# A gated attention kernel on one core: an up product moved ahead of the attention, the second Q moved behind the first scores, and the x pieces of the second half issued at other times

## The chip, the core and the metric

The kernel runs on one core of one Trainium2 chip. The core has four compute engines that work side by side: TensorE (PE, the matrix products), VectorE (DVE), ScalarE (ACT) and GpSimd (POOL); SyncE (SP) issues most of the transfers between the chip's main memory (DRAM) and the core's memory (SBUF). Products are written to PSUM, in banks of 128 x 512 numbers. Each engine takes its instructions strictly in the order in which they were written for it, and waits when the next one isn't ready.

The metric is the device time of one execution in microseconds, the median of several runs. The kernel before has 1978.97 us (three runs, 1977.46 to 1979.05).

## The reference

Input x is 2048 rows of 640. It is normalised by rows (xn), and the output is `x + s * g`:

```python
xn = _layernorm(x, axis=-1)
# s: 32 heads of 128, the last W = 512 keys and values of a cache of 2048
q = (xn @ wq); p = softmax(q @ k.T * 128**-0.5); s = concat_heads(p @ v) @ wo
# g: an MLP of width 1728 with a squared ReLU, then SiLU
h = xn @ w1 + b1; r = where(h > 0, h, 0); g = silu((r * r) @ w2 + b2)
```

All is done in float32. Every product of two float32 matrices is made of three products of shorter parts (hi x hi, hi x lo, lo x hi): the code calls that a triple. A part is made by a rounding copy (hi) and a subtraction (lo).

## The kernel before

The 2048 rows are four tiles of 512 columns (`NT`); 640 is five chunks of 128 (`DC`), 1728 is fourteen chunks f of up to 128 (`FC`). The work has three stages.

**The MLP of tiles 0 to 2** (`mlp_step`, L379). For each tile and chunk f: five triples of the up product, ReLU on ACT, square on POOL, split on ACT and DVE, then five triples of the down product. `gate` (L369) ends a tile. The normalised, split x of every tile is stored in DRAM (`xT_d`) for the attention.

**The attention** runs in 128 units: two halves of two tiles, each half with 16 groups of two heads, each group with two tiles, so four units to a group. For unit i:

- `q_mm` (L487): Q, 15 products from x (`ax`) and `wq` into a bank `pq`; `q_hi` and `q_lo` split it. Q is made two units ahead (`AHEAD`).
- `s_mm` (L510): scores, 12 products into four banks `s`.
- `max_fold`, `gather`, `row` (L521 to L553): maxima over the keys on DVE (`rdm`), gathered by ACT, reduced by DVE to `rowm`; SP stores the row as `m_d` in DRAM and reads it back as a broadcast to 128 partitions, `bm`.
- `shift` (L555): DVE subtracts `bm` from the scores in four steps and frees the four banks; the result is `e`. `expo`, `p_hi`, `p_lo` make exp and its parts `pt` (ACT, POOL), `s_add` the sum `su` (POOL, between the two `pt`).
- `s_fold`, `gather`, `row`: the sums, the same way with `rds`, `s_d` and the broadcast `bs`.
- `v_mm` (L588): 12 products into the only bank `o`; `o_norm` (DVE, times `bs`), `o_hi`, `o_lo` make `ot`. `r_mm` (L612) multiplies by `wo`, after every second unit, and `r_acc` adds up.

One unit comes to 54 products in the steady course.

**The MLP of tile 3** is spread over the rest. Chunks 11 to 13 are *early*: their up product (`early_up`, L727) is put among the first four units, with weights and x still in SBUF; `late_relu`, `late_square` (on DVE here) and `early_split` make h, which SP stores in DRAM (`h_d`) and reads back at the end (`late_h`, L749). Chunks 0 to 10 are *late*: weights are loaded and split again (`late_load`, `late_prep`), up products `late_up` and down products `late_down` are put among and after the last units, and for the five output columns d the down products of the early chunks, `late_gate` and the store end the kernel.

**The order is written out by hand.** Every step of the attention and of the late stage is put in a list by `at(when, step)` (L863), with a planned time; unit i starts at i times 12.4 (`PERIOD`). The list is sorted by planned time, and this gives each engine its order, SP's queue of transfers too. The planned times set the order alone; nothing waits for them.

The x of the second half (10 pieces of 256 KB a tile, two parts by five chunks) is loaded by L881 to L888 while the first half ends. Each tile takes over the SBUF room of a tile of the first half after that tile's last Q. The first tile's first use is the Q of unit 64, made in unit 62; the second tile's is the Q of unit 66, in unit 64.

Names in the profile: `eu` are the early products, `lu` and `ly` the late up and down products, `lr` the ReLU's result, `eh_x` and `eh_g` the two parts of an early h, `lh` the parts of h in the late stage, `l1w`, `l2w` its weights. Most instructions are recorded under line 72, that of a helper, so groups are told apart by these names.

Of the kernel before, what the change touches and what calls it, by code (L numbers as in the profile page):

```python
# [8 lines left out]
F32 = mybir.dt.float32  # L9
# [5 lines left out]
P = 128  # L15
NT = 512
# [4 lines left out]
def kernel(  # L21
# [62 lines left out]
    ]  # L84
    g_d = [dpool.tile([P, DC, NT], F32, name=f"g_d{t}") for t in range(LATE)]
    s_d = [dpool.tile([P, DC, NT], F32, name=f"s_d{t}") for t in range(NTILE // 2)]
    h_d = {f: dpool.tile([P, 2, NT], F32, name=f"h_d{f}") for f in range(FC - 3, FC)}

    def raw(ap):
        return ap.bitcast(F32)  # L90
# [7 lines left out]

    psx = ctx.enter_context(tc.tile_pool(name="psx", bufs=1, space=PSUM))

    FA = FC - 3
    keep = ctx.enter_context(tc.tile_pool(name="keep", bufs=1))
    mctx, wctx, hctx = ExitStack(), ExitStack(), ExitStack()
    wpa = wctx.enter_context(tc.tile_pool(name="mwa", bufs=1, side="right"))
# [5 lines left out]

    w1s, w2s = [], []
    for f, (f0, n) in enumerate(chunks):
        wp = wpa if f < FA else wpb
        if n < P:
            w1s.append([wp.tile([P, DC, 2 * n], F32R, name=f"w1s{f}")])
        else:
            if f < FA - 1:
                w1p = [wp.tile([P, DC, n], F32R, name=f"w1s{f}_{i}") for i in range(2)]
            else:
                two = keep.tile([P, 2, D], F32R, tag="ot", name=f"w1s{f}", bufs=4)  # L120
                w1p = [two[:, i, :].rearrange("p (c n) -> p c n", n=n) for i in range(2)]
            w1s.append(w1p)
        w2s.append([wp.tile([P, D], F32R, name=f"w2s{f}_{i}") for i in range(2)])
# [322 lines left out]
    def bank(name, k):  # L446
        return pools["psa"].tile([P, NT], F32, tag=f"qr{k}", name=name, bufs=1)
# [39 lines left out]
    def q_mm(i, cs):  # L487
        hf, g, t, h = units[i]
        if 0 in cs:
            QPS[i] = bank(f"pq{i}", int(i != 1))  # L490
        ws, xs = WQ[hf, h], XT[hf, t]
        for c in cs:
            triple(
                QPS[i],
                (ws[0][:, c, :], ws[1][:, c, :]),
                (xs[0][:, c, :], xs[1][:, c, :]),
                c == 0,
                c == DC - 1,
            )

    def q_hi(i):
        Q[i] = pair("q", [P, NT], f"q{i}", AHEAD + 1)
        act.activation(Q[i][0], QPS[i], AF.Copy, scale=SCALE)
# [243 lines left out]
            sp.dma_start(h_d[f][:, k, :], raw(h))  # L747

    def late_h(f):  # L749
        kind, bufs = ("wv", G) if f < FC - 1 else ("q", AHEAD + 1)  # L750
        LH[f] = pair(kind, [P, NT], f"lh{f}", bufs)
        for k in range(2):
            sp.dma_start(raw(LH[f][k]), h_d[f][:, k, :])

    def late_relu(f, kind):
        n = chunks[f][1]
# [55 lines left out]
        store(sp, HALF - 1, TPH - 1, d, a)  # L812

    steps_n = len(steps)
    opened = (LATE - 1) * FC + FA
    for n in range(steps_n):
        mlp_step(n)
        if n == opened:
# [28 lines left out]
            :, :NT  # L847
        ],
    )
    q_mm(1, range(DC))  # L850
    q_hi(1)
    q_lo(1)
    mctx.close()
    ap = ctx.enter_context(tc.tile_pool(name="at", bufs=2))
    pools["psb"] = ctx.enter_context(tc.tile_pool(name="psb", bufs=1, space=PSUM))
# [7 lines left out]
    def at(when, f, *a):  # L863
        plan.append((max(when, 0.0), len(plan), f, a))
# [14 lines left out]
                    at(base + when, prep, kind, hf, h)  # L879
    at(10.0, pad, pools["ep"], 480)  # L880
    for t in range(TPH):  # L881
        for c in range(DC):
            k, late = divmod(c + 1 - t, 2)
            w = (NG * UPG + t * G - 3 - AHEAD + t + k) * PERIOD + (8.5 if late else -1.6)
            if c == 0:
                at(w, open_xT, 1, t)
            for i in range(2):
                at(w + 0.7 * i, load_xT, 1, t, i, slice(c, c + 1))  # L888
    R_AT = (
        ((2 * PERIOD + 11.25, range(G)),),  # L890
        ((3 * PERIOD + 2.75, range(G)),),
# [9 lines left out]
    for i in range(NU):  # L901
# [5 lines left out]
        hf, g, t, h = units[i]  # L907
        for c in range(KC):
            on(0.68 * c, s_mm, i, c)
        if i + AHEAD < NU:  # L910
            q_at = 3.45 if i % G and i > UPG else 4.3
            for c in range(DC):
                on(q_at + 0.68 * c, q_mm, i + AHEAD, (c,))
            on(q_at + 3.5, q_hi, i + AHEAD)
            on(q_at + 4.1, q_lo, i + AHEAD)
        for c in range(KC):
            on(0.8 + 0.68 * c, max_fold, i, c)
        on(3.95, gather, i, "m")
# [40 lines left out]
    for item in order:  # L959
        kind, n = item[0], int(item[1:] or 0)  # L960
        if kind == "u":
            UP_AT[n] = now
        elif kind == "d":
            DOWN_AT[n] = now
            at(now, late_down, n, range(DC))
        elif kind == "r":
            at(now, r_mm, NU - 1, n, range(G), (n + 1) % 2)
            at(now + 1.36, r_acc, NU - 1, n)
        else:
            for k, d in enumerate(range(DC)):  # L970
                for f in range(FC - 3, FC):
                    DOWN_AT.setdefault(f, now)
                    at(now + 0.68 * (3 * k + f - FC + 3), late_down, f, (d,))
                at(now + 2.04 * (k + 1), late_gate, d)
        now += STEP[kind]
    PREP = {
        0: z - 2 * PERIOD + 8.4,
# [31 lines left out]
    for f, u in sorted(DOWN_AT.items()):  # L1009
# [3 lines left out]
        at(PREP2[f], late_prep, 2, f)  # L1013
        if f >= FA:
            at(now - 8.0 - 4.0 * (FC - f), late_h, f)
    EARLY_IN = (0,) * 7 + (1,) * 3 + (2,) * 3 + (3,) * 2
    for n, u in enumerate(EARLY_IN):
        k, c = divmod(n, DC)
        f = FA + k
        at(u * PERIOD + 8.0 + 0.01 * n, early_up, f, k % 2, c)  # L1020
        if c == DC - 1:
            at(u * PERIOD + 10.6, late_relu, f, "s")
            at(u * PERIOD + 12.0, late_square, f, dve)
            at((u + 1) * PERIOD + 7.6, early_split, f)
    at(z + 2.0, late_x)
    for d in range(DC):
# [51 lines left out]
```

## Time and profile before

| what | before |
|---|---|
| median of three runs | 1978.97 us |
| the profiled execution | 1978.84 us |
| its span, first to last instruction | 1977.1 us |
| PE busy | 1952.0 us (99%) |
| DVE, POOL, ACT busy | 1534.0, 1379.6, 1186.0 us |
| DRAM traffic over the span | 111 GB/s |
| granted TensorE clock, mean | 0.999 |

The page of the profile gives totals; the timeline gives every instruction with its start, its length, and in brackets how long its engine stood idle before it and for what. Engine names with a q (SPq) are the queues that issue transfers: the length there is that of issuing, not of moving the data. A stage view gives, for a stretch of the span, each engine's busy time and the rate at which the transfers moved data. A product of 512 columns is shown with 389 ns, but such products overlap; their distance is shorter.

### The profile page before, as it was taken

How to read it: one execution, taken by the hardware profiler on the slowest of the kernel's cores; microseconds unless marked ns; L12 is line 12 of the kernel's file. 1: busy time of each engine (PE TensorE's matmuls, PEld its weight loads, DVE VectorE, ACT ScalarE, POOL GpSimd, SP SyncE). 2: the span in 40 equal slices, each digit the busy share in tenths (PEclk: the TensorE clock that was granted, in tenths of full speed). 3: DMA queues.
4: the chain of work that ended last, by engine and by line, in shares of the span. 5: the costliest groups of instructions: out<-in, count | busy, mean ns of one | idle time of the engine just before them, and what ended most of it. 6: DMA issues, size and time to landing. Idle time of an engine off the chain costs nothing.

```text
span 1977.1 us, 25595 instructions
## 1 busy us (share of the span) xinstructions
PE 1952.0 (99%) x8576; PEld 1607.7 (81%) x8576; DVE 1534.0 (78%) x2638; ACT 1186.0 (60%) x2035; POOL 1379.6 (70%) x763
## 2 busy tenths in 40 slices
PE   7999999999999999999999999999999999999998
PEld 6888887888888888888887788888888888888877
DVE  5533336788888888888888878888888888888864
ACT  4432326766666666666666676666666666666643
POOL 2121225888888888888887788888888888888841
PEclk9999999999999999999999999999999999999999
DMA  5431444333233333333335533333333333323454
GB/s 150 125 112 33 181 178 147 107 91 91 92 92 91 91 93 90 95 92 92 91 97 166 160 97 107 113 114 115 112 114 113 113 112 113 97 91 92 110 156 133
DMA packets 128917, 220.35 MB, mean 111 GB/s; under 512 B 23590, under 2 KB 38352, under 8 KB 127504
## 3 DMA queue, kind: packets, MB, share of 16 engines
q1 hardware_dynamic: 125792, 204.28, 34.3%
q0 software_dynamic: 2992, 14.43, 1.8%
q8 instruction: 67, 1.10, 0.2%
q14 instruction: 66, 0.54, 0.1%
HBM read 194.26 MB, written 24.39 MB: 111 GB/s over the span
## 4 chain that ended last, share of the span: by engine, by line
PE 87%; DVE 5%; DMA 4%; ACT 2%; issue 1%; POOL 0%; SPq 0%; DVEq 0%; ACTq 0%; POOLq 0%
PE r L72 20%; PE pq L72 20%; PE o L72 16%; PE s L72 16%; PE ph L95 2%; PE ph L97 2%; PE ph L96 2%; PE py L96 2%; PE py L95 2%; PE py L97 2%; PE ly L72 2%; PE lu L72 1%; DMA w1r<-in_w_dram 1%; DVE acc L72 1%; DMA bm<-m_d 1%
## 5 line engine op out<-in xcount | busy, mean ns | idle before, releaser
L72 POOL TENSOR_TENSOR pt<-e,pt 128x1024 fp32r<-128x1024 f32 x256 | 616.3, 2407 | 128.7 <-ACT pt L72 101.9
L72 PE MATMUL r<-ot,wo 128*128 128x512 f32 x1920 | 497.0, 389 | 0.3 <-DVE acc L72 0.3
L72 PE MATMUL pq<-ax,wq 128*128 128x512 f32 x1920 | 456.5, 389 | 0.8 <-DMA ax<-xT_d 0.6
L72 PEld LDWEIGHTS pq<-ax,wq 128*128 128x128 f32 x1920 | 360.4, 188 | 76.2 <-DMA ax<-xT_d 1.5
L72 PEld LDWEIGHTS r<-ot,wo 128*128 128x128 f32 x1920 | 360.3, 188 | 75.8 <-DVE acc L72 0.7
L72 PE MATMUL s<-q,wk 128*128 128x512 f32 x1536 | 369.6, 389 | 4.6 <-DVE e L72 4.6
L72 PE MATMUL o<-pt,wv 128*128 128x512 f32 x1536 | 371.1, 390 | 0.8 <-DVE ot L72 0.5
L72 ACT ACTIVATE e<-e 128x1024 f32<-128x1024 f32 x256 | 269.7, 1053 | 136.7 <-DVE e L72 116.7
L72 DVE TRANSPOSE_TENSOR_REDUCE rdm<-s 128x16 f32<-128x512 f32 x512 | 343.0, 707 | 3.0 <-PE s L72 2.9
L72 PEld LDWEIGHTS s<-q,wk 128*128 128x128 f32 x1536 | 288.0, 188 | 66.3 <-DVE e L72 6.0
L72 PEld LDWEIGHTS o<-pt,wv 128*128 128x128 f32 x1536 | 287.3, 188 | 64.5 <-DVE ot L72 2.9
L72 DVE TENSOR_TENSOR e<-s,bm 128x512 f32<-128x512 f32 x512 | 312.5, 666 | 18.4 <-DMA bm<-m_d 18.2
L72 POOL TENSOR_TENSOR su<-e,e 128x1024 f32<-128x1024 f32 x128 | 307.8, 2405 | 0.0
L72 ACT ACTIVATE pt<-e 128x1024 fp32r<-128x1024 f32 x256 | 271.8, 1062 | 7.8
L72 DVE TENSOR_TENSOR acc<-r,acc 128x512 f32<-128x512 f32 x300 | 203.0, 677 | 8.9 <-PE r L72 8.6
L289 POOL TENSOR_TENSOR r<-r 128x512 f32<-128x512 f32 (+1 forms) x42 | 43.8, 1044 | 216.3 <-ACT r L330 194.5
L72 ACT ACTIVATE ot<-o 128x512 fp32r<-128x512 f32 x128 | 76.7, 599 | 172.3 <-DVE o L72 172.3
L72 DVE TRANSPOSE_TENSOR_REDUCE rds<-su 128x32 f32<-128x1024 f32 x128 | 158.3, 1237 | 1.6 <-POOL su L72 1.6
L72 DVE TENSOR_TENSOR ot<-o,ot 128x512 fp32r<-128x512 f32 x128 | 88.5, 692 | 85.1 <-ACT ot L72 85.1
L72 ACT ACTIVATE q<-pq 128x512 fp32r<-128x512 f32 x128 | 76.6, 599 | 105.3 <-PE pq L72 105.3
L72 POOL TENSOR_TENSOR wq<-qr,wq 128x640 fp32r<-128x640 f32 x62 | 97.7, 1576 | 55.1 <-ACT wq L72 55.1
L72 POOL TENSOR_TENSOR wv<-vr,wv 128x512 fp32r<-128x512 f32 x64 | 83.0, 1297 | 73.6 <-ACT wv L72 66.5
(127 smaller groups left out, 2163.1 us busy)
## 6 DMA issues: line engine op xcount, KB each, us to landing
bm<-m_d SPq DMA_DIRECT2D x128, 256.0 KB, 3.3
bs<-s_d SPq DMA_DIRECT2D x128, 256.0 KB, 4.0
qr<-in_wq_dram SPq DMA_DIRECT2D x64, 320.0 KB, 4.3
or<-in_wo_dram SPq DMA_DIRECT2D x64, 320.0 KB, 3.8
kr<-in_kT_dram SPq DMA_DIRECT2D x64, 256.0 KB, 4.0
vr<-in_v_dram SPq DMA_DIRECT2D x64, 256.0 KB, 4.3
xT_d<-xT POOLq DMA_DIRECT2D x6, 1280.0 KB, 7.7
xb<-in_x_dram SPq DMA_DIRECT2D x16, 320.0 KB, 3.7
```

The source lines that it names most:

```text
L72: ins = method(*args, **kwargs)
L95: nc.tensor.matmul(ps, ah, bh, start=first and i == 0, stop=False)
L96: nc.tensor.matmul(ps, ah, bl, start=False, stop=False)
L97: nc.tensor.matmul(ps, al, bh, start=False, stop=last and i == n - 1)
L289: nc.gpsimd.tensor_tensor(r, r, r, op=ALU.mult)
```

## The change

Four things are done:

- Chunk 10 becomes a fourth early chunk. Its up product (15 products) stands after the MLP of tile 2 and before the first scores. The early products are spread anew over units 0 to 3 (12, 12, 12 and 9 products, where it was 21, 9, 9 and 6), and their squares stand on DVE behind the maxima of a unit and before `rowm`. Chunk 10 is taken out of the late loop; the last part of the kernel has four down products for each column.
- The second Q (unit 1) moves from before the first scores to behind them; the third Q comes later in unit 0, with its `q_lo` in unit 1. All Q now use one PSUM bank.
- The x pieces of the second half: for each tile chunk 0 at 8.5 of a unit, then chunks 1 and 2 in the next unit and 3 and 4 in the one after, all at 4.2, which is right behind `m_d` and `bm` in SP's queue. Before, they were issued at two places of a unit, 8.5 and 10.8 (-1.6 of the next), the second ahead of `m_d`.
- Stored h is read back by one transfer of 512 KB for each chunk, into tiles `pt`, where it was two of 256 KB into others.

```diff
-    FA = FC - 3
+    FO, FA = FC - 3, FC - 4
...
-            QPS[i] = bank(f"pq{i}", int(i != 1))
+            QPS[i] = bank(f"pq{i}", 1)
...
     def late_h(f):
-        kind, bufs = ("wv", G) if f < FC - 1 else ("q", AHEAD + 1)
-        LH[f] = pair(kind, [P, NT], f"lh{f}", bufs)
-        for k in range(2):
-            sp.dma_start(raw(LH[f][k]), h_d[f][:, k, :])
+        two = ap.tile([P, 2, NT], F32R, tag=f"pt{f % 2}", name=f"lh{f}", bufs=3)
+        LH[f] = [two[:, k, :] for k in range(2)]
+        sp.dma_start(raw(two), h_d[f])
...
-    q_mm(1, range(DC))
-    q_hi(1)
-    q_lo(1)
+    EARLY_IN = (-1,) * 5 + (0,) * 4 + (1,) * 4 + (2,) * 4 + (3,) * 3
+    EARLY = [(FA + n // DC, n % DC) for n in range(len(EARLY_IN))]
+    for (f, c), u in zip(EARLY, EARLY_IN):
+        if u < 0:
+            early_up(f, 0, c)
...
     for t in range(TPH):
-        for c in range(DC):
-            k, late = divmod(c + 1 - t, 2)
-            w = (NG * UPG + t * G - 3 - AHEAD + t + k) * PERIOD + (8.5 if late else -1.6)
+        w = (NG * UPG + t * G - 3 - AHEAD) * PERIOD
+        for c, when in enumerate((8.5, *[PERIOD + 4.2] * 2, *[2 * PERIOD + 4.2] * 2)):
             if c == 0:
-                at(w, open_xT, 1, t)
+                at(w + when, open_xT, 1, t)
             for i in range(2):
-                at(w + 0.7 * i, load_xT, 1, t, i, slice(c, c + 1))
+                at(w + when + 0.01 * (2 * c + i), load_xT, 1, t, i, slice(c, c + 1))
...
-        if i + AHEAD < NU:
-            q_at = 3.45 if i % G and i > UPG else 4.3
+        qs = [(i + AHEAD, 3.45 if i % G and i > UPG else 4.3, 4.1)]
+        if i == 0:
+            qs = [(1, 2.8, 4.1), (2, 9.1, PERIOD - 5.2)]
+        elif i == 1:
+            qs = [(3, 4.2, 4.1)]
+        for n, q_at, low in qs if i + AHEAD < NU else ():
             for c in range(DC):
-                on(q_at + 0.68 * c, q_mm, i + AHEAD, (c,))
-            on(q_at + 3.5, q_hi, i + AHEAD)
-            on(q_at + 4.1, q_lo, i + AHEAD)
+                on(q_at + 0.68 * c, q_mm, n, (c,))
+            on(q_at + 3.5, q_hi, n)
+            on(q_at + low, q_lo, n)
...
             for k, d in enumerate(range(DC)):
-                for f in range(FC - 3, FC):
+                for f in range(FA, FC):
                     DOWN_AT.setdefault(f, now)
-                    at(now + 0.68 * (3 * k + f - FC + 3), late_down, f, (d,))
-                at(now + 2.04 * (k + 1), late_gate, d)
+                    at(now + 0.68 * ((FC - FA) * k + f - FA), late_down, f, (d,))
+                at(now + 0.68 * (FC - FA) * (k + 1), late_gate, d)
...
-    EARLY_IN = (0,) * 7 + (1,) * 3 + (2,) * 3 + (3,) * 2
-    for n, u in enumerate(EARLY_IN):
-        k, c = divmod(n, DC)
-        f = FA + k
-        at(u * PERIOD + 8.0 + 0.01 * n, early_up, f, k % 2, c)
+    for n, ((f, c), u) in enumerate(zip(EARLY, EARLY_IN)):
+        if u >= 0:
+            when = (6.3, 3.4 if EARLY_IN[n - 2] < u else 8.0, 8.0, 8.0)[u]
+            at(u * PERIOD + when + 0.01 * n, early_up, f, (f - FA) % 2, c)
         if c == DC - 1:
-            at(u * PERIOD + 10.6, late_relu, f, "s")
-            at(u * PERIOD + 12.0, late_square, f, dve)
+            at(u * PERIOD + 10.6 if u >= 0 else 0.3, late_relu, f, "s")
+            at((u + 1) * PERIOD + 3.97, late_square, f, dve)
             at((u + 1) * PERIOD + 7.6, early_split, f)
```

More of the change, by code (lines that the diff above doesn't have):

```diff
@@ L86 @@
     s_d = [dpool.tile([P, DC, NT], F32, name=f"s_d{t}") for t in range(NTILE // 2)]
-    h_d = {f: dpool.tile([P, 2, NT], F32, name=f"h_d{f}") for f in range(FC - 3, FC)}
+    h_d = {f: dpool.tile([P, 2, NT], F32, name=f"h_d{f}") for f in range(FC - 4, FC)}
     def raw(ap):
@@ L112 @@
     for f, (f0, n) in enumerate(chunks):
-        wp = wpa if f < FA else wpb
+        wp = wpa if f < FO else wpb
         if n < P:
@@ L116 @@
         else:
-            if f < FA - 1:
+            if f < FA:
                 w1p = [wp.tile([P, DC, n], F32R, name=f"w1s{f}_{i}") for i in range(2)]
@@ L814 @@
     steps_n = len(steps)
-    opened = (LATE - 1) * FC + FA
+    opened = (LATE - 1) * FC + FO
     for n in range(steps_n):
```

## The prediction

> **What bounds the kernel now.** I read the page first: the span and the chain that ended last.
>
> ```profile
> span 1977.1 us, 25595 instructions
> PE 87%; DVE 5%; DMA 4%; ACT 2%; issue 1%; POOL 0%; SPq 0%; DVEq 0%; ACTq 0%; POOLq 0%
> ```
>
> TensorE (PE) carries 87% of the chain. The change removes no product, so it can gain only where PE idles; I looked for such places with the stage view, one stretch per attention unit, cut at the first score product of each. Columns: stretch, its length, PE busy and its instructions, clock, DMA share, GB/s.
>
> ```profile
> 304.75:316.11 11.36, 11.04 (x49) 1.00 0.52 188
> 316.11:328.80 12.69, 11.32 (x49) 1.00 0.30 94
> 328.80:341.20 12.40, 11.41 (x48) 1.00 0.43 133
> 341.20:353.93 12.73, 12.28 (x52) 1.00 0.25 88
> 353.93:366.17 12.24, 12.24 (x56) 1.00 0.39 136
> 366.17:378.76 12.59, 12.56 (x56) 1.00 0.33 90
> 1027.89:1130.75 102.86, 99.92 (x433) 1.00 0.53 157
> 1142.99:1253.15 110.16, 110.16 (x487) 1.00 0.33 102
> ```
>
> An undisturbed unit takes 12.24 us for 54 products in the kernel's order, so a product costs 12.24/54 = 0.2267 us. The first four units hold 48, 48, 48 and 51 products (195, 44.21 us by that price) and take 49.18: **4.97 us idle at the start**. The last row is nine undisturbed units (9 x 12.24 = 110.16). The row above it is the eight units around the change of halves: 102.86 - 8 x 12.24 = **4.94 us lost there**. These 9.9 us are nearly all there is to win.
>
> What is late at the change of halves, from the timelines of SP, DVE and PE (start, length, engine, instruction):
>
> ```profile
> 335.07 0.33 SPq L72 DMA_DIRECT2D m_d<-rowm  x1
> 336.41 0.33 SPq L72 DMA_DIRECT2D bm<-m_d  x1
> ...
> 1055.19 0.90 SPq L72 DMA_DIRECT2D ax<-xT_d  x2
> 1058.02 0.32 SPq L72 DMA_DIRECT2D m_d<-rowm  x1
> 1061.63 0.32 SPq L72 DMA_DIRECT2D bm<-m_d  x1
> 1062.00 0.43 SPq L72 DMA_DIRECT2D ax<-xT_d  x1
> 1063.13 0.32 SPq L72 DMA_DIRECT2D s_d<-rows  x1
> 1066.04 0.32 SPq L72 DMA_DIRECT2D bs<-s_d  x1
> ```
> ```profile
> 1065.24 2.48 DVE L72 TENSOR_TENSOR e<-s,bm 128x512 f32<-128x512 f32 x4 [2.14 <-DMA bm<-m_d]
> ```
> ```profile
> 1100.11 1.37 PE L72 MATMUL pq<-ax,wq 128*128 128x512 f32 x3 [0.65 <-DMA ax<-xT_d]
> ```
>
> SP can issue the broadcast bm only when the row m_d has landed: 1.34 us in a quiet unit (335.07 to 336.41), 3.61 us behind two x pieces (1058.02 to 1061.63). DVE then waits 2.14 us for bm, and the next scores wait for DVE. Once PE waits for an x piece itself.
>
> **The change part by part.**
>
> *Late stage.* The up product of chunk 10, 15 products, leaves it: 15 x 0.2267 = **-3.40 us**, if PE stays the limit there.
>
> ```profile
> 1946.79 23.96 PE L72 MATMUL ly<-lh,l2w 128*128 128x512 f32 x105
> 1970.84 0.69 ACT L72 ACTIVATE lsg<-ly,b_sb 128x512 f32<-128x512 f32 x1 [1.40 <-PE ly L72]
> 1971.82 0.74 DVE L72 SCALAR_TENSOR_TENSOR acc<-ly,b_sb,acc 128x512 f32<-128x512 f32 x1
> ```
>
> The last 105 products run without a gap. Each gated column now has four triples, 12 x 0.2267 = 2.72 us, where it had 2.04. One thing gets tight: the last w2 weights wait for the down product of chunk 9, and are first used 9 products (2.04 us) later; a copy and a subtraction of ACT's and DVE's kind (0.69 and 0.74 above) make about 1.5, so it is hidden, and costs up to 0.3 if it is not. The reloads of h, now one 512 KB transfer for each chunk, start 12 us and more ahead. In the tail DVE was still adding when the sigmoid ended (1970.84 + 0.69 = 1971.53, next DVE step 1971.82); with 2.72 us a column it is free: **-0.3**.
>
> *Start.* The 15 products move in front of the first scores, and Q of unit 1 behind them. PE alone would hide all 15 in 4.97 us of idle time. But the idle time is there because the scores of unit i+1 wait for e(i), the subtraction of the maximum on DVE, so what counts is the distance from e to e.
>
> ```profile
> 328.05 2.48 DVE L72 TENSOR_TENSOR e<-s,bm 128x512 f32<-128x512 f32 x4 [0.25 <-DMA bm<-m_d]
> 338.07 1.21 DVE L72 TENSOR_TENSOR eh_g<-lr,eh_x 128x512 fp32r<-128x512 f32 x1
> 340.51 2.43 DVE L72 TENSOR_TENSOR e<-s,bm 128x512 f32<-128x512 f32 x4
> 351.99 2.48 DVE L72 TENSOR_TENSOR e<-s,bm 128x512 f32<-128x512 f32 x4
> 364.90 2.43 DVE L72 TENSOR_TENSOR e<-s,bm 128x512 f32<-128x512 f32 x4
> ```
> ```profile
> 331.61 2.41 POOL L72 TENSOR_TENSOR pt<-e,pt 128x1024 fp32r<-128x1024 f32 x1 [0.80 <-ACT pt L72]
> 333.97 2.40 POOL L72 TENSOR_TENSOR su<-e,e 128x1024 f32<-128x1024 f32 x1
> 336.32 2.41 POOL L72 TENSOR_TENSOR pt<-e,pt 128x1024 fp32r<-128x1024 f32 x1
> ...
> 1881.19 2.39 POOL L72 TENSOR_TENSOR pt<-e,pt 128x1024 fp32r<-128x1024 f32 x1 [5.04 <-ACT pt L72]
> 1883.53 2.87 POOL L72 TENSOR_TENSOR su<-e,e 128x1024 f32<-128x1024 f32 x1
> ```
> ```profile
> 1881.61 2.52 DVE L72 TENSOR_TENSOR lh<-lr,lh 128x512 fp32r<-128x512 f32 x1 [0.95 <-ACT lh L72]
> ```
>
> The three distances are 12.46, 11.48 and 12.91 us. The short one has neither a square (lr) nor a split (eh_g) of an early product. These DVE steps read two SBUF tensors, as POOL's do, and the rows show them waiting: eh_g from 338.07 ends at 339.28, 0.55 us after POOL's pt (336.32 + 2.41 = 338.73); lh from 1881.61 ends at 1884.13, 0.56 after pt (1883.58), and POOL's next su took 2.87 us instead of 2.40. After the change units 2, 3 and 4 all have both, and the square stands behind the maxima, while POOL's first pt runs: it waits for pt's end and pushes su, the second pt and so eh_g by 0.47. That makes 12.46 + 0.47 = 12.9, as much for the unit that had 11.48, and 12.91 + 0.47 = 13.4: 39.2 against 36.85, or 2.4 later. In the row at 364.90 e had 1.27 us to the scores at 366.17, of which one of its four subtractions needs 2.43/4 = 0.6, about 0.75 with the handovers: 0.5 is absorbed. 2.4 - 0.5 gives **+1.9 us** here, against the 3.40 won later. e(1) I leave at 328.05: the square that stood ahead of its maxima is gone, its scores come about 0.9 later. The second Q's bank is wanted by the fourth Q right behind its last read; one fold and one subtraction, some 1.6 us by the DVE steps above, stand against two triples put between (1.36), so PE waits about 0.3, which ends before e(1). The early store of h sits on SP behind bm, ahead of weights used a unit later. Bounds: -1.57, when the 210 products (47.61 us) run without idle time, to +3.40, when all 15 lie on the path.
>
> *Change of halves.* The pieces go from ahead of m_d to behind bm, four a unit (once five, a piece of the second tile being in front of the sums' row too). So m_d finds a quiet queue, but s_d, the row of sums, stands behind them.
>
> ```profile
> 1048.00:1050.00 2.00, 2.00 (x10) 1.65 (x10) 1.75 (x4) 1.58 (x5) 0.53 (x1) 1.00 0.41 110
> 1050.00:1052.00 2.00, 2.00 (x11) 1.65 (x10) 1.12 (x4) 0.78 (x2) 1.77 (x2) 1.00 0.53 166
> 1058.00:1060.00 2.00, 2.00 (x10) 1.65 (x10) 1.30 (x2) 1.20 (x2) 2.00 (x2) 1.00 1.03 400
> ```
> ```profile
> bs<-s_d SPq DMA_DIRECT2D x128, 256.0 KB, 4.0
> ```
> ```profile
> 1037.79 0.32 SPq L72 DMA_DIRECT2D s_d<-rows  x1
> ```
> ```profile
> 1045.56 0.68 DVE L72 TENSOR_TENSOR o<-o,bs 128x512 f32<-128x512 f32 x1
> ```
>
> The rows are the DMA rate (last column) while a broadcast is moved, with one piece behind it, and with pieces and weights alone. After the change: bm at 110 GB/s takes 2.4 us, four pieces (1.05 MB) at 400 take 2.6; with about 0.9 to start, the queue is empty 5.9 us after bm, and a row needs about 1 more. s_d comes 5.11 us after m_d (1058.02 to 1063.13), so 3.8 after bm: it waits 3.1 us, 3.8 with five pieces; before it waited 2.91 (1063.13 to 1066.04). DVE uses bs 7.77 us after s_d (1037.79 to 1045.56), bs takes 4.0, so 3.8 are allowed: it just fits. But bs comes nearly 2 us later than in a quiet unit (1.34), and the weights behind it reach towards the next m_d. I leave a quarter of the 4.94 in place (about 0.3 for each of four units), nearer to the full gain since the waits fit: **-3.6**, bounds 0 and -4.94; a loss beyond is the last rival.
>
> *Sum*, against the profiled execution (1978.84 us): 1978.84 - 3.40 - 0.3 + 1.9 - 3.6 = **1973.4**. That run is 0.13 below the median of those shown, which I let stand.
>
> **The rivals.** (1) POOL and DVE do not get in each other's way at the start, and the halves gain all: 1978.84 - 3.40 - 0.3 - 4.94 = 1970.2; for it speaks that a square can fall into a pause of POOL, against it the back-to-back POOL rows. (2) The pieces only move the jam: bs is late, its weights with it, the next m_d waits as before: 1978.84 - 3.40 - 0.3 + 1.9 = 1977.0; for it, the stretch already moves 157 GB/s and no byte is saved. (3) The added product lies on the start's path entirely: 1978.84 - 0.3 - 3.6 = 1974.9; for it, e, not PE, sets those units. (4) Slower: the four pieces drain at the 166 GB/s seen with one piece behind a broadcast. They take 6.3 us instead of 2.6, s_d waits 6.8, DVE stands 3.0 us before the output's normalisation in each of four units: 1978.84 - 3.40 - 0.3 + 1.9 + 4 x 3.0 - 4.94 = 1984.1. The time is longer than before once a unit stands over (4.94 + 1.8)/4 = 1.7 us, which is below about 210 GB/s. The 400 GB/s row speaks against it. The Trainium skill (DMA: Bandwidth & Descriptors, "Two DMAs through the same engine are not ordered") says that descriptors of one queue start in order: s_d cannot pass the pieces. The same page ("Measured") has 6.15 us for 1 MB issued from GpSimd; by that figure, an estimate, rival 4 would come true. The 400 GB/s of this trace decides for me.
>
> **How the numbers follow.** Forecast 0.52, rivals 0.13, 0.17, 0.10, 0.08. 0.2% (3.96 us) is about what a measurement of this kernel can tell from no change: faster means below 1975.0, slower above 1982.9. Faster: the forecast but 0.05 of it, rival 1, half of rival 3, whose time lies on the line: 0.47 + 0.13 + 0.05 = 0.65. Same: the rest of these and rival 2, 0.05 + 0.05 + 0.17 = 0.27. Slower: rival 4, 0.08. The range, 1970.0 to 1979.0, takes in rivals 1, 2 and 3 and leaves out rival 4 and the far ends.
>
> **What would show it.** In the profile after: units 2 to 4 with e to e near 13, squares of 1 us and more, su of 2.87; the eight units around the halves near 99 instead of 102.86, with m_d to bm back under 2 us and s_d to bs near 3; the late products still without a gap; the last gate free of DVE's backlog. It is wrong if bs holds DVE for over a microsecond, or the late stage waits for weights.

## The result, and the profile after

The changed kernel takes 1981.03 us (median of 22 runs, 1978.98 to 1983.83), the kernel before 1978.57 us on the same chip (22 runs, 1976.49 to 1979.84). The ratio is 1.0014 [1.0008, 1.0021]: 2.5 us slower, where 5.4 us faster was forecast. It lies outside the forecast's range.

The profiled execution of after (1983.69 us, span 1981.9 us) is 4.85 us longer than that of before; it is the second slowest of the 22, so some 2.4 us of this belong to the execution and not to the kernel. The groups of instructions say which products wait more. Last part of each row: idle time of TensorE just before the group, and what ended most of it. First before, then after:

```profile
L72 PE MATMUL r<-ot,wo 128*128 128x512 f32 x1920 | 497.0, 389 | 0.3 <-DVE acc L72 0.3
...
L72 PE MATMUL s<-q,wk 128*128 128x512 f32 x1536 | 369.6, 389 | 4.6 <-DVE e L72 4.6
L72 PE MATMUL o<-pt,wv 128*128 128x512 f32 x1536 | 371.1, 390 | 0.8 <-DVE ot L72 0.5
```

```profile
L72 PE MATMUL r<-ot,wo 128*128 128x512 f32 x1920 | 497.0, 389 | 1.6 <-DVE acc L72 1.6
...
L72 PE MATMUL s<-q,wk 128*128 128x512 f32 x1536 | 369.9, 390 | 5.5 <-DVE e L72 5.5
L72 PE MATMUL o<-pt,wv 128*128 128x512 f32 x1536 | 371.6, 390 | 3.5 <-DVE ot L72 2.5
```

The scores (s) and above all the products with the values (o) wait longer: o waits for `ot`, which is made after the normalisation by `bs`, the broadcast of the sums. (In the eleven units around the change of halves, which the next view shows, it is the scores that gain most: TensorE's wait before `s` goes from 1.9 to 4.5 us, before `o` from 0.2 to 2.2.) Where in time, the stage view tells, cut at the first score product of units 0, 7, 59, 70 and 127 (stretch, length, PE busy). Before, then after:

```profile
304.75:391.00 86.25, 83.10 (x359) 66.31 (x357) 65.64 (x111) 60.11 (x106) 63.85 (x38) 1.00 0.35 116
1027.89:1167.47 139.58, 136.64 (x595) 110.95 (x594) 114.06 (x200) 90.58 (x160) 109.10 (x56) 1.00 0.49 145
1865.36:1977.10 111.74, 104.30 (x456) 84.64 (x454) 64.74 (x88) 44.25 (x70) 38.85 (x25) 0.99 0.48 146
```

```profile
304.98:393.45 88.47, 86.32 (x374) 69.05 (x373) 71.74 (x113) 60.58 (x108) 65.04 (x38) 1.00 0.38 120
1029.98:1174.82 144.84, 138.08 (x596) 110.53 (x594) 113.62 (x200) 90.05 (x160) 108.79 (x56) 1.00 0.47 140
1872.87:1981.90 109.03, 100.76 (x441) 81.82 (x439) 63.55 (x87) 42.29 (x67) 35.61 (x23) 0.99 0.49 151
```

Start: +2.22 us. Change of halves (eleven units): +5.26. Last unit and late stage: -2.71. The stretches between add 0.03, in all 4.80, the difference of the spans. Start and late stage came as forecast in sign and nearly in size; the change of halves was forecast at -3.6 and got worse by more than what there was to win.

What happens there is seen in SP's queue and in VectorE (DVE) of after, in the unit that issues five pieces:

```profile
1060.27 0.33 SPq L72 DMA_DIRECT2D m_d<-rowm  x1
1062.01 0.33 SPq L72 DMA_DIRECT2D bm<-m_d  x1
1062.38 2.52 SPq L72 DMA_DIRECT2D ax<-xT_d  x5
1065.45 0.32 SPq L72 DMA_DIRECT2D s_d<-rows  x1
1070.09 0.33 SPq L72 DMA_DIRECT2D bs<-s_d  x1
```

```profile
1066.69 2.48 DVE L72 TENSOR_TENSOR e<-s,bm 128x512 f32<-128x512 f32 x4 [1.27 <-DMA bm<-m_d]
...
1081.30 2.48 DVE L72 TENSOR_TENSOR e<-s,bm 128x512 f32<-128x512 f32 x4 [2.25 <-DMA bm<-m_d]
...
1089.29 0.70 DVE L72 TENSOR_TENSOR o<-o,bs 128x512 f32<-128x512 f32 x1 [1.16 <-DMA bs<-s_d]
```

`m_d` to `bm` is short here (1.74 us), as forecast. But `bm` itself, issued at 1062.01, is used at 1066.69, 4.68 us later, where in before, with one piece behind it, it took 3.61 (1061.63 to 1065.24). The row of sums leaves at 1065.45 and has landed at 1070.09, 4.64 us later, forecast 3.8 with five pieces. DVE waits 1.27 us for this `bm` and 2.25 us for the next, and then 1.16 us before the normalisation, over the microsecond that the prediction named as a sign of being wrong. The DMA rate (last column) behind `bm`:

```profile
1062.00:1064.00 2.00, 2.00 (x11) 1.60 (x9) 2.00 (x3) 0.57 (x3) 2.00 (x1) 1.00 0.46 70
1064.00:1066.00 2.00, 2.00 (x10) 1.46 (x9) 1.35 (x5) 1.58 (x4) 1.12 (x2) 1.00 0.89 162
1066.00:1068.00 2.00, 1.59 (x7) 1.01 (x6) 1.31 (x3) 0.00 (x0) 1.87 (x2) 1.00 1.04 391
1068.00:1070.00 2.00, 2.00 (x10) 1.64 (x9) 2.00 (x4) 1.90 (x2) 0.00 (x0) 1.00 0.45 169
```

In the first two stretches, with the broadcast under way, broadcast and pieces together move 70 and 162 GB/s, in the third the pieces run at 391. In half-microsecond stretches the rate is at most 152 up to 1065.5 and 311 to 410 from there to 1068.5: the pieces are at full rate over a microsecond before DVE gets `bm`.

### The profile page after: what moved, and what is told of

It is laid out like the page before. It is cut to its first block, busy times and chain, and to the rows that moved or that the text cites. A ratio compares the mean times of both kernels' runs of the same rounds, so it can differ in the third digit from the quotient of the medians.

```text
span 1981.9 us, 25593 instructions
## 1 busy us (share of the span) xinstructions
PE 1952.8 (99%) x8576; PEld 1606.9 (81%) x8576; DVE 1540.2 (78%) x2639; ACT 1184.0 (60%) x2034; POOL 1377.1 (69%) x761
## 4 chain that ended last, share of the span: by engine, by line
PE 73%; DMA 3%; DVE 3%; ACT 2%; issue 1%; POOL 0%; SPq 0%; ACTq 0%; POOLq 0%; DVEq 0%
PE r L72 20%; PE pq L72 19%; PE o L72 16%; PE s L72 15%; PE ly L72 2%; DMA bm<-m_d 1%; DMA m_d<-rowm 1%; PE lu L72 1%; ACT e L72 1%; DVE e L72 1%; ACT pt L72 1%; ACT rdm L72 0%; DMA l2r<-in_w_dram 0%; DVE acc L72 0%; DVE rdm L72 0%
```

## The experiments

**Theory:** the pieces right behind `bm` slow `bm` and hold the row of sums, and this alone turns the forecast around. **Rival:** the early product costs more than the late stage wins, and the pieces do little. The experiments ran on four chips (e1 to e4 on one, e5 to e12, e13 to e15 and e16 on one each), where before stands at 1975.9 to 1976.3 us; each ratio is to before on the same chip. The stages are read as above, one profile each. "Lost" is the eleven units' length less 11 x 12.24 us; the column behind it says how much of that lies in the last five of them, units 65 to 69; "end" is from the last unit's first score to the end. The profiles of the result above lost 4.94 (0.17 of it in units 65 to 69) before and 10.20 (4.15) after.

| kernel | median us | ratio to before | units 0 to 7 | lost, 59 to 70 | in 65 to 69 | end |
|---|---|---|---|---|---|---|
| e5_before_again | 1976.07 | 1.0003 [0.9994, 1.0011] | 85.80 | 4.32 | 0.27 | 111.12 |
| e10_after_again | 1979.96 | 1.0021 [1.0012, 1.0030] | 88.50 | 8.39 | 3.67 | 108.09 |
| e1_pieces_alone | 1978.93 | 1.0015 [1.0007, 1.0024] | 85.78 | 7.57 | 1.53 | 110.59 |
| e2_old_pieces | 1978.03 | 1.0011 [1.0002, 1.0020] | 88.49 | 6.14 | 3.27 | 107.59 |
| e3_pieces_between | 1976.28 | 0.9999 [0.9990, 1.0008] | 88.46 | 3.60 | 3.43 | 108.12 |
| e12_half_the_pieces | 1973.88 | 0.9988 [0.9979, 0.9997] | 88.44 | 2.65 | 2.65 | 107.38 |
| e4_act_square | 1975.51 | 0.9999 [0.9990, 1.0007] | 87.26 | 4.87 | 2.31 | 108.39 |
| e13_start_alone | 1981.72 | 1.0027 [1.0017, 1.0036] | 88.46 | 6.92 | 3.24 | 110.88 |
| e14_q_order_alone | 1980.81 | 1.0019 [1.0010, 1.0028] | 88.95 | 4.36 | 0.00 | 111.66 |
| e9_late_alone | 1973.05 | 0.9984 [0.9975, 0.9993] | 85.90 | 3.01 | 0.23 | 107.88 |
| e6_between_act_square | 1975.00 | 0.9993 [0.9984, 1.0002] | 87.37 | 4.27 | 3.71 | 108.63 |
| e7_between_alone | 1974.26 | 0.9992 [0.9983, 1.0001] | 85.64 | 3.09 | 2.99 | 111.17 |
| e11_stores_alone | 1976.39 | 1.0004 [0.9995, 1.0013] | 85.66 | 4.42 | 0.03 | 111.31 |
| e15_order_and_places | 1976.24 | 1.0000 [0.9991, 1.0009] | 90.45 | 0.96 | 0.09 | 110.68 |
| e8_stores_between | 1972.51 | 0.9980 [0.9971, 0.9988] | 88.32 | 2.27 | 1.59 | 107.66 |
| e16_places_on_before | 1972.25 | 0.9982 [0.9973, 0.9991] | 86.09 | 0.42 | 0.42 | 110.42 |

### What one profile is worth: both kernels again

> The kernel before, unchanged, once more with a profile of its own: what one profile of it is worth. If its first profile is typical, the ratio lies between 0.9995 and 1.0005, the first seven units take 86.0 to 86.5 us, units 59 to 70 lose 4 to 6 us against eleven units of 12.24 us, and the last unit's first score stands 111 to 112.5 us before the end. The rival: the first profile caught a slow end. Then the last distance is 110 us or less, and 1 to 2 us of the late gain that was forecast were never there.

> The changed kernel once more, unchanged, on the same chip as the runs beside it. Its first comparison gave 1.0014 [1.0008, 1.0021], its first profile lost 10.2 us in units 59 to 70. If that profile is typical, the loss is 8.5 to 11 us again, with bm to its first shift at 4.3 to 4.7 us in units 60 to 63, and the ratio is 1.0008 to 1.0022. The rival: pieces and start cost add up as e1_pieces_alone (1.0015) and e2_old_pieces (1.0011) have them singly: then 1.0023 to 1.0030.

Before repeats itself within its interval; its first seven units are a little shorter than expected (85.80). Its profiled execution here lies 2.4 us above its median (1978.48), so the spans of two profiles do not tell kernels apart to better than that; single stages repeat more closely, start and end within 1 us, the change of halves within 0.6 for before (4.94, 4.32) and 1.8 for after (10.20, 8.39). After is 3.9 us slower than before on this chip, at the upper end of what was expected; the loss, 8.39, lies just under.

### The halves: pieces alone, old pieces, half the bytes

The first puts the new piece places into before, the second the old ones into after. The third is after with this edit:

```diff
-            for i in range(2)
-        ]
+            for i in range(2 - hf)
+        ] * (1 + hf)
...
-            for i in range(2):
+            for i in range(1):
                 at(w + when + 0.01 * (2 * c + i), load_xT, 1, t, i, slice(c, c + 1))
```

> The kernel before with the new places of the x pieces alone. Theory: the four or five pieces right behind bm slow bm itself (4.3 to 4.7 us from issue to the first use in the profile after, against 3.5) and hold back the row s_d (3.9 to 6.3 us to bs, against 1.3 to 3.1), so the units around the change of halves lose about 9 us instead of 4.9, and the time is 2 to 5 us above before (ratio 1.0010 to 1.0025). Rival: the extra loss of the profile after came from rows that were late for another reason in the units behind the pieces; then this kernel loses 5 us or less there and its ratio is 0.9985 to 1.0003.

> The kernel after with the x pieces at their places of before, so the early product and the moved Q alone. Theory: the start gives about 2 us up and the late stage wins 3.4 and the tail 0.3, so the time is 1 to 2.5 us below before (ratio 0.9988 to 0.9996), and the units around the change of halves lose about 4.9 us, as before. Rival: the early product costs as much at the start as it wins late, ratio 0.9998 or more.

> After with half of the pieces' bytes: in the second half of the units the low part of x is neither loaded nor kept, and the high part is used in its place (so the output is another one). Places in the queue stay: two transfers of 256 KB behind each of those broadcasts in place of four. If it is the bytes behind a broadcast that slow it and hold the next row, bm to its first shift falls from 4.3 to 4.7 us to 3.5 to 4.1 us in units 60 to 63, the s_d behind the pieces waits under 3 us in place of 3.9 to 6.3, the loss in units 59 to 70 falls to 3 to 6.5 us, and the time lies 2.5 to 6 us under e10_after_again. The rival, the place in the queue and not the bytes: the loss stays 8.5 to 11 us and the time within 1 us of e10_after_again.

Pieces alone: 3.0 us slower and 7.57 us lost in the eleven units; the theory's time, and somewhat less than the 9 us that it named. Half the bytes, at the same places of the queue: 6.1 us under after, and only 2.65 us are lost, even less than expected, all of it in units 65 to 69. SP's queue at the same place as above, three pieces in place of five:

```profile
1057.83 0.32 SPq L72 DMA_DIRECT2D m_d<-rowm  x1
1059.21 0.33 SPq L72 DMA_DIRECT2D bm<-m_d  x1
1059.58 1.38 SPq L72 DMA_DIRECT2D ax<-xT_d  x3
1062.80 0.32 SPq L72 DMA_DIRECT2D s_d<-rows  x1
1065.41 0.32 SPq L72 DMA_DIRECT2D bs<-s_d  x1
```

`s_d` waits 2.61 us in place of 4.64, and `bm`, issued at 1059.21, is used at 1063.30, after 4.09 us. So it is what follows a broadcast that delays it and the row. Bytes and number of transfers were halved together here, so this run does not tell these two apart. SP's time for issuing them is not the cause: `s_d` leaves 3.44 us after `bm` with five pieces, 3.59 with three. The second run went against the theory: after with the old places is no faster than before, but 2.1 us slower. Something else in the change costs too; that is the next part.

### The start: alone, without the new product, without the lock

e13 is before with only the new start; e14 is before with only the second Q behind the first scores. e4 is e2 with the early squares on ACT, right behind their ReLU:

```diff
-            at((u + 1) * PERIOD + 3.97, late_square, f, dve)
+            at(u * PERIOD + 10.65 if u >= 0 else 0.35, late_square, f, act)
```

> Before with the start of after alone: four early up products, the second Q behind the first scores, pieces and late stage as in before (the late stage makes chunk 10's h again, and the early one is stored and not read). This is the start's cost without what it buys, plus nothing else. By the profiles the first seven units take 2.5 us more (88.5 against 85.9): if that is the whole cost, the ratio is 1.0008 to 1.0018. The rival: the medians of e2_old_pieces and e9_late_alone, which differ by this start alone, stand 5.0 us apart, so the start also makes the change of halves worse: then 1.0019 to 1.0028, with 6 us or more lost in units 59 to 70.

> Before with the second Q (15 products) moved behind the first scores, as in after, and nothing put in its place: three early products, as before. The first scores then begin 3.4 us earlier. If the first units are set by the distance from one subtraction of the maximum to the next, and the second Q fits into time in which TensorE waits, nearly all of it is won: 1.5 to 3.4 us, a ratio of 0.9983 to 0.9992; and the start's term is this gain less the price of the added product (3.4 us and the locks). The rival: the distance grows by the Q's products, and the ratio is 0.9996 to 1.0005.

> The kernel with the x pieces as before, and the early squares moved from DVE to ACT, right behind their ReLU. Theory: the square on DVE waits for POOL's first pt and pushes POOL's su by 0.47 us, so without it su is 2.40 again in units 2 to 4, the distances from e to e fall from 13.8, 13.0 and 13.3 us to about 12.5 each, and the time is 1 to 2 us below the kernel with the old pieces (ratio 0.9980 to 0.9990 against before). Rival: the chain is long for another reason (the split alone, or ACT, which gets 0.7 us more a unit); the distances stay near 13 and the time is that of the kernel with the old pieces.

The start alone costs 5.4 us, the rival's value. Of this the first seven units show 2.2 to 2.7 (88.46 against 86.25 and 85.80) and the change of halves 2.0 to 2.6 (6.92 against 4.94 and 4.32). SP's order in these units is the same, and the extra of the second part lies in units 65 to 68, which take 12.86 to 13.34 us. What is late there are the rows of maxima of units 65 and 67, each behind two stores of accumulators. SP's queue in unit 67, before and then e13:

```profile
1135.74 0.32 SPq L72 DMA_DIRECT2D m_d<-rowm  x1
1138.07 0.32 SPq L72 DMA_DIRECT2D bm<-m_d  x1
```

```profile
1137.76 0.32 SPq L72 DMA_DIRECT2D m_d<-rowm  x1
1141.58 0.32 SPq L72 DMA_DIRECT2D bm<-m_d  x1
```

From `m_d` to `bm` it takes 2.33 us in before and 3.82 in e13 (1.97 and 3.24 in unit 65). The trace's records of transfers show something at this row that no step of the kernel issues: a load of 16 KB of instructions. In all nine profiles of kernels with the new start one begins 0.15 to 1.98 us after unit 67's `m_d`, and the row takes 2.92 to 4.56 us. In the other nine it begins about 5 us after `m_d`, or none is near, and the row takes 1.80 to 2.33 us, except in e1 and e7 (2.96 and 3.04). The last section shows what such a load goes along with in undisturbed units. So the second part goes along with where these loads fall; no run here moves one alone, so it is not shown that they make all of it, nor why the new start puts them there.

e14 fell out contrary to what both theories said: moving the second Q alone wins nothing and costs 4.5 us, of which the profile's first seven units show 2.7 to 3.2. TensorE's timeline shows why, at the first scores:

```profile
304.66 1.65 PE L72 MATMUL s<-q,wk 128*128 128x512 f32 x6 [2.77 <-DVE sgl L374]
```

The first scores do not start earlier without the Q in front of them. They wait for DVE's last gate of tile 2 (`sgl`), 2.77 us; the Q's 15 products (3.40 us) stood there nearly for nothing. In after, the first 15 early products take over that shelter, and the second Q goes into the units:

```profile
301.58 3.56 PE L72 MATMUL eu<-xT,w1s 128*128 128x512 f32 x15
304.98 1.30 PE L72 MATMUL s<-q,wk 128*128 128x512 f32 x5
```

So the change really moves 15 products into the units: 359 products became 374, PE busy 83.10 became 86.32, and of these 3.22 us only 1.0 came out of idle time.

The lock of POOL and DVE came out as forecast. DVE and POOL of after in unit 1:

```profile
327.32 2.43 DVE L72 TENSOR_TENSOR e<-s,bm 128x512 f32<-128x512 f32 x4
332.66 2.02 DVE L72 TENSOR_TENSOR lr<-lr 128x512 f32<-128x512 f32 x1
338.15 1.71 DVE L72 TENSOR_TENSOR eh_g<-lr,eh_x 128x512 fp32r<-128x512 f32 x1
341.09 2.43 DVE L72 TENSOR_TENSOR e<-s,bm 128x512 f32<-128x512 f32 x4
```

```profile
331.73 2.40 POOL L72 TENSOR_TENSOR pt<-e,pt 128x1024 fp32r<-128x1024 f32 x1
334.08 2.86 POOL L72 TENSOR_TENSOR su<-e,e 128x1024 f32<-128x1024 f32 x1
336.91 2.40 POOL L72 TENSOR_TENSOR pt<-e,pt 128x1024 fp32r<-128x1024 f32 x1
```

The square ends at 334.68, 0.55 us after POOL's `pt` (334.13), and POOL's `su` takes 2.86 us. The split `eh_g` ends at 339.86, again 0.55 after `pt` (339.31). With the squares on ACT:

```profile
326.12 2.43 DVE L72 TENSOR_TENSOR e<-s,bm 128x512 f32<-128x512 f32 x4
...
339.55 2.43 DVE L72 TENSOR_TENSOR e<-s,bm 128x512 f32<-128x512 f32 x4
```

```profile
333.00 2.41 POOL L72 TENSOR_TENSOR su<-e,e 128x1024 f32<-128x1024 f32 x1
```

`su` is back at 2.41, the first distance from e to e 13.43 in place of 13.77; the three sum to 38.81 in place of 40.04 (13.43, 12.52 and 12.86; about 12.5 each was expected). The seven units win 1.2 us, the median 2.5 against e2; a little more than expected. Beside before this gives 0.9999 and not 0.9980 to 0.9990, since e2 was slower than thought.

### The late stage alone

This is the late stage of after on the start of before; `late_h` loads `h_d[max(f, FO)]`.

> Before with the late stage of after alone: the start, the order of the Qs and the places of the pieces are those of before; the fourth late product is left out and the stored result of its neighbour is loaded and used in its place (so this part of the output is another one). This is the late gain without what pays for it. If the forecast's late and tail terms are right (3.7 us together), the time lies 2.7 to 4.2 us under before: a ratio of 0.9979 to 0.9987. The rival: the new late stage gives back part of it in new waits (the residual product waits for VectorE's accumulation, behind the last broadcast of sums): then 0.5 to 2 us, 0.9990 to 0.9998.

```profile
1862.92:1970.80 107.88, 100.83 (x441) 81.81 (x439) 63.24 (x87) 42.41 (x67) 35.85 (x23) 0.99 0.50 153
```

The end is 3.2 to 3.9 us shorter than in before's two profiles, the median 3.1 us lower: the late gain is real, and near the forecast.

### Other places for the pieces and the accumulators' stores

e3 and e7 issue the pieces in `row`, between a row's store and its broadcast, on the start of after and of before. e8 and e11 move the ten stores of the accumulators (`s_d<-acc`) there too; they had stood ahead of a row's store, waiting for DVE. e6 is e3 with the squares on ACT, e8 builds on it; e16 is before with both places, e15 the same on e14. The edit with both, without the list of units and pieces that fills `BETWEEN`:

```diff
         sp.dma_start(d, r)
+        while what == "m" and PEND:
+            t, c = PEND.pop(0)
+            sp.dma_start(s_d[t][:, c, :], ACC[0, t][:, c, :])
+        for t, k, c in BETWEEN.pop((i, what), ()):
+            if k == 0 and c == 0:
+                open_xT(1, t)
+            load_xT(1, t, k, slice(c, c + 1))
         bc = ap.tile([P, NT], F32, tag=f"b{what}", name=f"b{what}{i}", bufs=2)
...
-            sp.dma_start(s_d[t][:, d, :], ACC[hf, t][:, d, :])
+            PEND.append((t, d))
```

> The kernel after with the x pieces issued between a row and its broadcast (two behind m_d and ahead of bm, two or three behind s_d and ahead of bs), when the queue stands empty for over a microsecond anyway. Theory: what costs is the pieces ahead of a row and right behind a broadcast, not their bytes; m_d to bm and s_d to bs stay near 1.4 us and the loss around the change of halves falls from about 10 us in the profile after to under 4, for a ratio of 0.9975 to 0.9990 against before. Rival: the bytes set it, since bm, bs, weights and pieces fill the queue; the loss stays at 5 us or more, ratio 0.9995 to 1.0015.

> The two repairs together: pieces between a row's store and its broadcast, and the early squares on ScalarE. If their gains add up (2.5 us for the square, 1.75 us for the pieces, both measured against e2_old_pieces, which stood at 1978.0 us), this gives 1973.5 to 1975 us beside a before of 1975.9 us: a ratio of 0.9985 to 0.9995, with less than 4.5 us lost in units 59 to 70. The rival: the two don't add up, since what the start wins is waited for later; then the ratio is 0.9997 to 1.0003.

> e6_between_act_square, and the ten stores of the accumulators (s_d<-acc) issued behind the next maximum row's store instead of where VectorE's addition is recorded: there they stand in SP's queue ahead of a row's store and wait for VectorE. If this is what still costs units 64 to 69 their 3 to 4 us, each m_d to bm takes under 2 us, the loss in units 59 to 70 falls under 1.5 us, and the ratio is 0.9968 to 0.9983. The rival: those units are late because of the transfers themselves (256 KB each, beside the broadcast), wherever they are issued: then the loss stays 2.5 to 4 us and the time within 0.7 us of e6_between_act_square.

> Before with one thing changed: the pieces of the second half issued between a row's store and its broadcast, in the time in which SP would only wait for the row to land. On the start of after (e3_pieces_between beside e2_old_pieces) this won 1.75 us. If it does the same on the start of before, the loss in units 59 to 70 is under 4 us in place of 4.3 to 4.9 and the ratio 0.9986 to 0.9995. The rival: the pieces were no burden to before where they stood, and what is late there are the accumulators' stores: then 0.9997 to 1.0004.

> Before with one thing changed: the ten stores of the accumulators issued behind the next maximum row's store, pieces and start as they were. If these stores, in front of a row's store in SP's queue, are what costs most of the 4.3 to 4.9 us that before loses in units 59 to 70, the loss falls to 1 to 3 us and the ratio is 0.9984 to 0.9993. The rival: without moving the pieces the same units wait for these; the loss stays over 3.5 us and the ratio 0.9996 to 1.0003.

> e14_q_order_alone with the pieces between a row's store and its broadcast and the accumulators' stores behind the next maximum row's store (e7_between_alone and e11_stores_alone had these singly on the start of before: 0.9992 and 1.0004; together, on the other start, e8_stores_between had 0.9980). If the parts add up, 0.9970 to 0.9984, with 1 to 2.5 us lost in units 59 to 70. The rival, that they do not add up: 0.9986 to 0.9996.

> Before with only the two new places in SP's queue: the pieces between a row's store and its broadcast, the accumulators' stores behind the next maximum row's store; start, second Q and late stage as before. Singly they gave 0.9992 and 1.0004, but e15_order_and_places lies 4.6 us under e14_q_order_alone, which differs by these two places. If they only work together, since each alone leaves the other transfers ahead of a row, the loss in units 59 to 70 falls under 2 us from 4.3 to 4.9 and the ratio is 0.9975 to 0.9988. The rival: 4.6 us was mostly the spread of the second-Q kernels' start, and the ratio here is 0.9990 to 0.9998.

SP's queue in e3, in the unit shown above:

```profile
1058.76 0.32 SPq L72 DMA_DIRECT2D m_d<-rowm  x1
1059.13 0.89 SPq L72 DMA_DIRECT2D ax<-xT_d  x2
1060.13 0.37 SPq L72 DMA_DIRECT2D bm<-m_d  x1
1063.73 0.32 SPq L72 DMA_DIRECT2D s_d<-rows  x1
1064.10 0.89 SPq L72 DMA_DIRECT2D ax<-xT_d  x2
1065.10 0.36 SPq L72 DMA_DIRECT2D bs<-s_d  x1
```

Two pieces are issued while SP would only wait for the row, which goes ahead of them and lands 1.37 us after its issue (1058.76 to 1060.13), as in a quiet unit. `bs` goes out before the pieces have drained, and no unit up to 63 is late. What is left (3.60 us) lies in units 64 to 68. The time was not as low as expected in e3, since the start's cost was still in it; e6 fits the sum of the two repairs. In e8 the stores win another 2.5 us, but units 67 and 68 stay at 12.92 and 13.08, so its loss is above the 1.5 expected.

On the start of before, the pieces' place alone wins 1.8 us (an interval that just takes in no change), the stores' place alone nothing, both together 3.6. The eleven units of e16:

```profile
1026.19:1161.25 135.06, 135.02 (x595) 111.43 (x594) 114.75 (x200) 90.59 (x160) 109.05 (x56) 1.00 0.46 150
```

0.42 us is lost where before lost 4.94 and 4.32, and the DMA rate is 150 GB/s where it was 145: the same bytes, in other places and in a shorter time. e15 fits neither of its expectations; the eleven units do (0.96 lost), but its start took 90.45 us (last section). e16 and e8 are both about 3.6 us faster than before and some 7.5 us faster than after (1979.96); e16 changes the two places and nothing else. So with the queue in order the moved up product buys nothing more: e8, which has it, is no faster beside before than e16 (0.9980 and 0.9982). e7 also shows that the places hang together: with the pieces out of the way, units 59 to 64 lose 0.10 us in place of 4.1 to 4.8, but units 65 to 69, late by 0.2 to 0.3 in before, now lose 2.99.

## Why the prediction failed, step by step

- **Late stage, -3.40, and tail, -0.3: right in kind, up to 1 us too large.** -2.71 in after's profile, -3.1 by the median of e9. PE's busy time fell by 3.54 us as counted, and the late products ran without a gap. Part of it went into a wait that the forecast had not: the residual products of the last unit wait 1.61 us for DVE's addition (0.32 before, in the same timeline), 1.08 in after's second profile. What holds DVE there was not followed up. In the tail, DVE now starts 0.72 us after the last sigmoid's start (0.98 before), so 0.26 of the 0.3 came.

```profile
1910.87 4.37 PE L72 MATMUL r<-ot,wo 128*128 128x512 f32 x18 [1.61 <-DVE acc L72]
...
1975.40 0.69 ACT L72 ACTIVATE lsg<-ly,b_sb 128x512 f32<-128x512 f32 x1 [2.08 <-PE ly L72]
1976.12 0.75 DVE L72 SCALAR_TENSOR_TENSOR acc<-ly,b_sb,acc 128x512 f32<-128x512 f32 x1 [0.56 <-ACT lsg L72]
```

- **Start, +1.9: right where it looked, +2.2 measured.** The distances are 13.77, 12.97 and 13.30 us, forecast 12.9, 12.9 and 13.4; squares, splits and `su` show the lock as worked out. What it did not see: with the old piece places, the kernels with the new start lose 2.3 to 3.3 us in units 65 to 69 (e2, e4, e13), those without it 0.0 to 0.3 (both profiles of before, e9, e11, e14). By medians the start costs 5.4 us. The late rows of units 65 and 67 go along with loads of instructions that begin there; what causes this second part stays open.
- **Change of halves, -3.6: wrong, and this is the step that failed.** "bm at 110 GB/s takes 2.4 us, four pieces at 400 take 2.6", with 0.9 to start, lets the broadcast be done in 3.3 us whatever stands behind it. The runs showed that the pieces behind it make it later: `bm` is used 4.3 to 4.7 us after its issue in units 60 to 63, 3.4 to 3.6 in before. The pieces drain later too, the row of sums behind them lands after 3.9 to 6.3 us in place of 3.1 to 3.8, and "it just fits" had no reserve for that. Then the weights behind `bs` reach into the next `m_d`, 3.06 and 2.79 us in units 62 and 63. In all, from a row's store to the use of its broadcast, these four units take 6.3, 6.4, 7.8 and 7.4 us, and took 6.1, 7.2, 5.8 and 6.9 in before: only in the second of them is it shorter, and nothing came of the 3.6. The pieces alone (e1) cost 3.0 us by medians. Of the +5.26 in the profile of after, 1.28 lies in units 59 to 64 and 3.98 in units 65 to 69, most of which the new start shows without the pieces (3.24 in e13). The bounds of this term, 0 and -4.94, were the second fault: the prediction itself named the loss as a rival, but kept it out of the range.
- **The rivals.** Rival 4 is nearest to what happened: slower, by the pieces behind the broadcast. Its size, 4 x 3.0 us, was too large; the term came to +5.26 in place of +7.1, and not all of that is the pieces'. Its path was another: it let the pieces drain at 166 GB/s, but they ran at 311 to 410 from 1065.5 on. And most of the lateness goes through `bm` and the next `m_d` to the subtraction (in the eleven units DVE waits 10.2 us for `bm`, 7.1 in before), less through the normalisation (1.7 us for `bs`, none in before). The Trainium skill's figure that spoke for it (DMA: Bandwidth & Descriptors, "Measured": 6.15 us for 1 MB) gives for the five pieces (1.25 MB) an estimate of 7.7 us. From their first issue (1062.38) to the landing of the row behind them (1070.09) it took 7.7 as well, but this time also holds the broadcast ahead of them and the row's own way, so the agreement is in part chance. Rival 2 (the jam only moves) was the milder form. The lock could not be taken away whole (rival 1); e4 shows 1.2 us of it.
- **The chances.** The gain seemed likely because 400 GB/s was seen for the pieces. That rate came again, once the broadcast was nearly through; what it does not tell is how late the broadcast itself becomes. The prediction quotes a row with a hint of that: `bs`, a broadcast of the same size with two loads of weights behind it, lands after 4.0 us in the median; `bm` of before lands after 3.3.

## What to carry to other kernels

A transfer's time belongs to what else is in flight: when transfers are put right behind another, look for a row in which both are under way, and expect the first one to land later too, not only the last. Before moving work out of the way of one small transfer, write down what then stands ahead of the next small one, and give it more reserve than a few tenths; the place that worked here was the issuer's own idle time, between a row's store and its read. And work ahead of a stage may sit in a shelter that only a wait provides: look at what its consumer waits for when it is gone, as the second Q's place showed. Last, see in which units the time is lost, before the whole of a stage is put down to one cause: a part of it lay in units after the last piece.

## What the runs showed of the hardware

**A broadcast of one row and plain loads slow each other down.** `bm`, 256 KB read from a 2 KB row, takes 3.61 us from its issue to its use with one 256 KB load behind it, 4.09 with three and 4.68 with five, DVE waiting for it each time. While `bm` is moved, the rate of both together stays at 152 GB/s or less (after, 1062.0 to 1065.5); then the loads run at 311 to 410.

**A row that meets a load of instructions lands later.** The profile of before lists a queue "instruction" with 67 transfers, 1.10 MB in all, so 16 KB each. In units 8 to 57 and 72 to 118 of all 18 profiles, a row of 2 KB (`m_d` to `bm`) takes 1.34 us in the median of the 1375 rows with no such load near, at most 2.25; in the 73 rows where one begins within a microsecond after the row's issue it takes 2.61 us in the median, 2.09 to 3.48.

**A short pause of TensorE can cost its clock.** In e14 and e15 TensorE waits 2.77 us before the first scores. The stage views of the 12 products behind this pause, e15 and then e14 (third column from the end: granted clock):

```profile
303.97:308.41 4.44, 4.44 (x12) 3.49 (x13) 2.16 (x3) 0.00 (x0) 0.97 (x6) 0.62 0.80 322
```

```profile
304.66:307.40 2.74, 2.74 (x12) 2.29 (x13) 1.75 (x3) 0.00 (x0) 0.97 (x6) 1.00 1.01 403
```

Up to here the two kernels have the same code. It ran at a mean granted clock of 0.62 in one execution (0.5 for 3.41 us, from 304.68 on) and 1.00 in the other, which makes 1.70 us, about what e15's start (90.45 us) is longer than e14's (88.95). The Trainium skill (TensorE: Matmul & The Clock Gate, "The HAM clock gate") says that the clock is halved after an idle window of about 3.4 us, and that the window runs freely, so that the loss varies from run to run; the variation agrees, and a pause of 2.77 us was enough here. In before and after TensorE has work there and no pause.
